# Score masks off TensorE, part of the normalising on GpSimd, and small matmuls between the first transposes, in a kernel of two attention and token-mixing layers

## The chip, the cores and the metric

The kernel runs as one program on one core of a Trainium2 chip. The metric is device time in microseconds, the median of the runs shown. Five engines work side by side: TensorE (PE in the profile, its weight loads apart as PEld), VectorE (DVE), ScalarE (ACT), GpSimd (POOL) and SyncE (SP), which here only issues DMAs. Each takes its own instructions strictly in order, and they wait for one another by semaphores.

## The reference, cut to what matters

```python
def _A_ref(x, wqkv, wo):                      # B=1, S=2048, D=512
    H = 32; Dh = 16; W = 256
    q, k, v = split(x @ wqkv)                 # (B, H, S, Dh) each
    scores = einsum("bhqd,bhkd->bhqk", q, k) * Dh ** -0.5
    mask = (i - j >= 0) & (i - j < W)         # causal, window of 256 keys
    p = softmax(where(mask, scores, -1e9))
    return reshape(einsum("bhqk,bhkd->bhqd", p, v)) @ wo
def _B_ref(x, w1, b1, w2, b2):                # mixes along the 2048 tokens; F = 1792
    u = gelu(einsum("bsd,sf->bdf", layernorm(x), w1) + b1)
    return transpose(einsum("bdf,fs->bds", u, w2) + b2)
for _ in range(2):                            # the same weights both times
    x = x + _A_ref(layernorm(x), A_wqkv, A_wo)
    x = x + _B_ref(layernorm(x), B_w1, B_b1, B_w2, B_b2)
```

Everything arrives as bf16. There are 32 heads of 16 columns, so a score matmul uses few rows of the array.

## The kernel before, in words

The 2048 tokens are 16 tiles of 128 rows that stay in SBUF. For attention, each layer goes through chunks of queries (layer 0: two of 256 queries, then three of 512; layer 1: four of 512), and through four groups of eight heads in each.

**A score group** (`f_sc`, L710) is the unit of the attention stage: some 8 to 24 small matmuls that fill four PSUM banks (two tiles of two banks). ScalarE then takes the exponential in two instructions (L736, "exp"), which write the probabilities to one of seven tiles of `pt`. A layer has 76 score groups, numbered 0 to 75 here, and so 152 exps. Blocks on the edge of the window hold scores that must not count. They are dealt with in one of two ways: GpSimd multiplies the probabilities by 0 or 1 after the exp (`f_mask`, L757), or TensorE adds a large negative bias to the scores before it, by extra matmuls of a selector with a bias table (L721). `BIASED` says which groups take the second way: in layer 0 two of each five groups in chunk 2 and in chunk 3, and eight of the ten groups in chunk 1; in layer 1 none. Then come the products with V ("PV", `f_pv`, L774, one per several score groups and 64 to 96 matmuls each), VectorE's transpose of the result (L794), the reciprocal (L798), a product with it on VectorE or GpSimd (L800), a second transpose (L805), the output projection and the residual (L816).

**Before attention** each pair of tiles is normalised: statistics (`stat` L492, `agg` L494) on VectorE, the power -1/2 on GpSimd (`rstd` L505), and the normalising itself (`normalise`, `xh`, L512) on VectorE. In layer 0 the first four tiles are transposed by TensorE (L570), evicted (`evt`, L577 on VectorE or L579 on ScalarE), and projected to K, Q and V (L534, a line shared by all the plain matmuls). K is spread into a zero-padded layout: from PSUM (`evka`, L602 on ScalarE or L603 on VectorE) in the first chunk, later by way of a staging tile (`evk` L614 or L616, then `kz`: L629 on GpSimd or VectorE, or eight DMAs at L624). The other tiles are transposed by DMA (`tr`, L563).

**The token mixing** is dense: `fu` and `ful` matmuls with w1 (L534 and L895, 128x512), the gelu on ScalarE (L910), `fy` matmuls with w2, and a residual (L936). `u_part` lets a share of the w1 matmuls run while attention goes on, as soon as their tokens have passed attention: they fill TensorE's gaps.

**What sets the order.** The code first makes a list of about 2,400 operations with their dependencies, some with a second or third engine that may take them (`alts`). `ORDER` is a packed list that gives the sequence of all operations and the engine of each; `replay` walks it, hands out buffers in that sequence and fills the engines' queues. So the order within each engine is fixed by `ORDER` alone. PSUM has eight banks in one pool, which score groups, PV sums and all other matmul outputs share.

**The start.** VectorE writes a tile of ones and `f_warm` issues 42 matmuls of 128 columns on it (L395), whose result nobody reads, while the first tokens are loaded.

Of the kernel before, what the change touches and what calls it, by code (L numbers as in the profile page):

```python
# [11 lines left out]
P = 128  # L12
# [15 lines left out]
    'Lc6t+<;M3LzFfBX`U0>1fEJ6AfmuFSET@ZtF)%La7=UrJ2}bqls8$1kBfBekI9yD1IoC9)>}SFOj}XB)>-O&;>=#KQb)_uIFt)O!i_H<nol=i1p%7CTg;_Q0'
    'R<c$%%i19boodag1MYfGvs(2;O5JL;&W8hs*K0x|8jS5K%drEYKECS%lQ^cR_49K_t6C6ZHqrg*G`PGBdIcD(*Ur_|KQ->yg7K=U8pdW5U)WKkYjLcGmTQS3'
    'Y1ok+;?~ubt{M98&jG)^k^R43se(cm4O(9<mkUbgA|q{8`Jnu6P>x0;H*hDO=eW~yOrW#SEK!i<e7-39L=mLw!SPO_I-R2YvUibQ;=EVIdEmO^F&=l_K~|=e'  # L30
    'h6%<7fr!}k_%@Dx&#hkgLCaq{#72&72SH5;RW)l?P1p5=*t%{IP=D)r)Kgs7kY)Ws5RZrsQC(8gFm6Xw9y_)xi(Uu?J2g!)Wzb@A+<>9RDO6~k)l{|sz?*Kj'
    'TQr#f{n{ZIsVtYNyqGT~!Twn~o6g`VoQy@F(QpU`Vdy2jZjx2{{Z<jhu4Q$_TV$gnhwUKsyk@<oyKW^-JvWKH7)Hp}bwg+m)OEpco3_~*L`|+jRfdoPfe^%w'
    'wS{mxxfBm~7Tv5j&AhAteYMi<RVrGaZjHw0<Kb#)>3Ugy^G%)`gP~}g3P_5qAU}XMwBN^;l{gDG-^oeXj^fDr_FLcgEVOZb&oSjc8W2DNA)>SZLZ?PIK;j7l'
    'Qr1ghFHL|@tDV{aAbYckswh+eghG(brY&u}U5oM(!bJiy8YAH(8b#T!*TsLm=vxM8Hd{?SYBZV+N-zYnnYeM1c1$OAfnkV3HUiVqEV+PyF;T;YX%Wj7osI~x'
    'u||Zr!or0s8lTYN8=WwPh{O=l-U(4|ZZH=n<VSd8;UHvwm<T-yhf_9TO!Qbfh@uFtI-M}g$E;H(JPgyc*G(tA-e?rxcGEN|Hk(l1xe3_;j?;7+;sM$1&=!f1'
    '<)9SSGVF%vL%<G9A<eqsIEI0c2*I!o3ur3P02T3LfOata684$+Jlearyrld5>~D|m-*!K&d2&8nPL78p>Evlc@pSJXZ1;co?$^9N*ZmYcsZ`!oo{jH4Pag&='
    'A3tBE@;E8pdV0U)*)gAjl>{r{{(RyG@2?O@$A0jz&(Q{llZ(;Mjy+F~A$ljBoV*C?4JeOMl)xU=hZjl@FRq*(N4$%$a)|R)^al^=kfz72KAObm=Xgc|Ns>N+'
    'VL#(@Qh95pa#E>$5{IS7xSp6LNtMIRBO9e-8t;7`;@?9Gq{r~2iX<JURC=D@r<#yHHChS$s`i^tb9?`jvz2=q9jax|s7I*3c=C9>JS}@8bEo&PL-55Hp9Ao@'
    'bfD5bxCdgtqSS$<(lL^vBq4lMf)nuKcBdR?JN?*~)QMQU7n*xzd8uE*Pd))}7s|6Lsys)ca#U=)%kF!xr=L}h)>Xg(5a}&q+)q5kBos$H?67(Fv}!-Q`;*?i'
    '+YRmp#1DcOT67PCw8u#Vzencu<mBxV1g|EghtpR+0?6y9O64)ehj1$|rMB|AmmHKtdaH`0=jsOzJbAGkNXJ?wN&i#HNv}mvdXQO3l3o&VuO5;FB<WZM_JdD)'  # L40
    '@^Ie6*zxGW@v-~8Ao)*pub+?PztWmVG5>#5{FgB4r{5%j2gDxiS@nEeiho_z{SPfNNM8'
# [52 lines left out]
class Graph:  # L94
# [4 lines left out]
    def __init__(self, nc, es):  # L99
        self.nc = nc  # L100
        self.sem = {e: es.enter_context(nc.semaphore(f"s_{e}")) for e in self.ENGS}
        self.dsem = [es.enter_context(nc.semaphore(f"s_dma{i}")) for i in range(self.NDMA)]
        self.ops = []
        self.last_w = {}
        self.readers = {}

    def op(self, eng, fn, reads=(), writes=(), cost=200.0, prio=None, dma=False, after=(), holds=(), cfg=None, cls=None,
# [20 lines left out]
        for k in writes:  # L128
            w = self.last_w.get(k)
            if w is not None:  # L130
                deps[w.idx] = w
            for rd in self.readers.get(k, ()):
                deps[rd.idx] = rd
        for a in after:
# [170 lines left out]
def bass_interleave_layers__sliding_block__mixer_token_mlp__prompt_kernel(  # L305
# [25 lines left out]
    BIASED = [{1: (0, 1), 2: (2, 4), 3: (2, 4)}, {}]  # L331
# [4 lines left out]
    with es:  # L336
# [679 lines left out]
```

## Time and profile before

| what | us |
|---|---|
| median of 3 runs (444.0 to 444.46) | 444.34 |
| the profiled execution: its time | 445.56 |
| the profiled execution: its span, first to last instruction | 443.6 |
| busy: PE, ACT, DVE, POOL | 418.5, 322.7, 307.4, 201.1 |
| layer 0, attention: from 11 to 159 us, PE busy, ACT busy | 134.93, 143.01 |
| layer 0, token mixing: from 159 to 205 us, PE busy, ACT busy | 45.12, 14.09 |
| layer 1, attention: from 205 to 365 us, PE busy, ACT busy | 155.09, 150.72 |
| layer 1, token mixing: from 365 to 443.6 us, PE busy, ACT busy | 75.24, 11.01 |

Read the table by stage. TensorE is the busiest engine over the whole span, but in layer 0's attention ScalarE is. The mean granted TensorE clock is 0.996 of full speed.

### The profile page before, as it was taken

To read this page: it belongs to the slowest core of one execution; us is meant where nothing else is said; L and a number is where in the kernel's file an instruction comes from. 1 tells how busy PE (TensorE), PEld (TensorE's weight loads), DVE (VectorE), ACT (ScalarE), POOL (GpSimd) and SP (SyncE) were. 2 spreads that over 40 slices of the span, in tenths; PEclk is the share of its full clock that TensorE was granted. 3 is DMA by queue.
4 is the path that set the end of the run, shared out by engine and by line. 5 is a ranking of instruction groups with operands and counts; after the bars stand their busy time and mean duration, and the time that the engine had idled before them with its cause. 6 is when DMAs were issued, how large, how long until landed. Compare 5 with 4: busy or idle time off the path is not lost.

```text
span 443.6 us, 14491 instructions
## 1 busy us (share of the span) xinstructions
PE 418.5 (94%) x6270; PEld 193.5 (44%) x6344; DVE 307.4 (69%) x582; ACT 322.7 (73%) x372; POOL 201.1 (45%) x305
## 2 busy tenths in 40 slices
PE   7888988998999999999999999999999999999997
PEld 5554443443443444444444444444334444444443
DVE  7988879777895678664468789898887457521223
ACT  3999999999999940708989999999999980430000
POOL 3567652464577641001456686677866551000000
PEclk8999999999999999999999999999999999999999
DMA  7575504410133538451434434031211347653533
GB/s 242 153 129 91 101 16 72 77 28 18 36 83 100 122 88 249 125 168 25 99 80 104 111 73 97 17 71 38 56 45 30 105 123 202 189 158 99 167 115 105
DMA packets 94127, 44.47 MB, mean 100 GB/s; under 512 B 24304, under 2 KB 94064, under 8 KB 94064
## 3 DMA queue, kind: packets, MB, share of 16 engines
q1 hardware_dynamic: 94064, 43.55, 39.1%
q8 instruction: 50, 0.82, 0.8%
q14 instruction: 13, 0.11, 0.1%
HBM read 33.56 MB, written 2.10 MB: 80 GB/s over the span
## 4 chain that ended last, share of the span: by engine, by line
PE 79%; ACT 13%; DVE 3%; issue 2%; DMA 1%; SPq 1%; POOL 1%; POOLq 0%
PE PS L534 53%; ACT pt L736 12%; PE PS L710 9%; PE PS L895 8%; PE PS L774 8%; DMA w1b<-in_B_w_dram 1%; DVE rl L794 1%; PE PS L721 1%; DVE stats L492 1%; SPq L830 1%; PE PS L570 0%; DVE vst L649 0%; DVE bb L472 0%; DVE x_sb L816 0%; POOL rstd L505 0%
## 5 line engine op out<-in xcount | busy, mean ns | idle before, releaser
L736 ACT ACTIVATE pt<-PS 128x1024 bf16<-128x1024 f32 (+1 forms) x304 | 281.9, 1034 | 12.0 <-PE PS L710 8.0
L757 POOL TENSOR_TENSOR pt<-pt,ldm 128x256 int32<-128x256 int32 (+2 forms) x226 | 146.9, 675 | 91.7 <-ACT pt L736 91.2
L534 PE MATMUL PS<-xhT,wqkv 128*128 128x512 bf16 (+1 forms) x267 | 65.3, 362 | 4.5 <-issue 1.4
L534 PE MATMUL PS<-xh_sb,w1b 128*128 128x512 bf16 x262 | 66.0, 380 | 2.9 <-issue 1.9
L534 PE MATMUL PS<-uT,w2b 128*128 128x512 bf16 (+1 forms) x285 | 66.7, 370 | 0.8 <-issue 0.5
L710 PE MATMUL PS<-qT,kbd 32*128 32x256 bf16 (+4 forms) x1488 | 60.4, 252 | 5.6 <-ACT pt L736 2.8
L936 DVE SCALAR_TENSOR_TENSOR x_sb<-PS,b2col,x_sb 128x512 bf16<-128x512 f32 x31 | 22.4, 745 | 48.4 <-PE PS L534 48.4
L505 POOL TENSOR_TENSOR rstd<-agg,mhalf 128x2 f32<-128x2 f32 (+1 forms) x33 | 23.5, 713 | 67.8 <-DVE agg L494 67.8
L794 DVE STREAM_TRANSPOSE rl<-PS 128x1024 f32<-128x1024 f32 x32 | 39.9, 1246 | 19.8 <-PE PS L774 19.3
L710 PEld LDWEIGHTS PS<-qT,kbd 32*128 32x128 bf16 x1488 | 22.0, 93 | 63.9 <-ACT pt L736 48.2
L774 PE MATMUL PS<-pt,vb 64*17 64x320 bf16 (+4 forms) x2976 | 43.6, 252 | 1.2 <-DVE vst L649 0.5
L910 ACT ACTIVATE uT<-rl,b1col 128x512 bf16<-128x512 f32 x28 | 18.5, 713 | 36.1 <-DVE rl L906 35.7
L492 DVE BATCH_NORM_STATS2 stats<-x_sb 128x6 f32<-128x512 bf16 x64 | 42.8, 678 | 0.4
L534 PEld LDWEIGHTS PS<-uT,w2b 128*128 128x128 bf16 x294 | 27.1, 98 | 30.9 <-issue 3.7
L534 PE MATMUL PS<-uT,pt 128*128 128x512 bf16 x163 | 39.5, 380 | 0.3
L774 PEld LDWEIGHTS PS<-pt,vb 64*17 64x17 bf16 x2976 | 31.0, 85 | 17.4 <-issue 7.3
L895 PE MATMUL PS<-xh_sb,w1b 128*128 128x512 bf16 x164 | 37.0, 379 | 0.7 <-DMA w1b<-in_B_w_dram 0.6
L534 PEld LDWEIGHTS PS<-xh_sb,w1b 128*128 128x128 bf16 x280 | 23.8, 98 | 31.6 <-issue 7.0
L534 PEld LDWEIGHTS PS<-xhT,wqkv 128*128 128x128 bf16 x288 | 24.5, 99 | 28.8 <-issue 5.6
L534 PE MATMUL PS<-wqkv,xhT 128*128 128x512 bf16 x115 | 32.3, 381 | 3.5 <-issue 1.3
L534 PE MATMUL PS<-wo_sb,oT 128*128 128x512 bf16 x124 | 32.6, 380 | 0.4 <-issue 0.3
L512 DVE TENSOR_SCALAR xh_sb<-x_sb,agg,rstd 128x512 bf16<-128x512 bf16 x64 | 27.2, 445 | 3.2 <-POOL rstd L505 3.1
(64 smaller groups left out, 337.0 us busy)
## 6 DMA issues: line engine op xcount, KB each, us to landing
w1b<-in_B_w_dram SPq DMA_DIRECT2D x112, 128.0 KB, 2.7
w2b<-in_B_w_dram SPq DMA_DIRECT2D x70, 128.0 KB, 2.6
pt<-in_B_w_dram SPq DMA_DIRECT2D x42, 128.0 KB, 3.2
vb<-vst SPq DMA_DIRECT2D x64, 68.0 KB, 2.1
out_dram<-x_sb SPq DMA_DIRECT2D x15, 128.0 KB, 1.8
x_sb<-in_A_x_dram SPq DMA_DIRECT2D x3, 512.0 KB, 7.3
wqkv<-in_A_wqkv_dram SPq DMA_DIRECT2D x4, 256.0 KB, 4.5
wqkv<-in_A_wqkv_dram SPq DMA_DIRECT2D x1, 512.0 KB, 6.6
```

What stands on the lines that cost most here:

```text
L492: op("vector:stat", lambda e: e.bn_stats(st[:, 0:6], x_sb[:, t, :]), reads=[f"x{t}"], writes=[("st", i)], cost=dve_cost(512))
L505: op("gpsimd:rstd", lambda e: e.tensor_tensor(rstd[:, t0:t1, 0], agg[:, t0:t1, 1], mhalf[:, 0:1].to_broadcast([P, t1 - t0]), op=ALU.pow), ...
L512: op("vector:xh", lambda e: e.tensor_scalar(xh_sb[:, t, :], x_sb[:, t, :], agg[:, t, 0:1], rstd[:, t, :], op0=ALU.subtract, op1=ALU.mult), ...
L534: return e.matmul(o, lhsT=w, rhs=x, start=start, stop=stop, skip_group_check=True)
L710: last = e.matmul(bank(tt[r // 2], r % 2)[:, base + c0 * 64:base + (c0 + n) * 64], lhsT=kbd[32 * r:32 * r + 32, tk.slot, o, jj].rearrange( ...
L736: op("scalar:exp", lambda e, ts=ts, tp=tp, i=i, cols=cols: e.activation(probs(tp)[:, i, 0:cols, :], pair(ts)[:, :, 0:cols].rearrange("p r ...
L757: return e.tensor_tensor(v, v, m, op=ALU.mult)
L774: last = e.matmul(bank(t, h)[32 * r:32 * r + 17, i + q0 * 64:i + (q0 + n) * 64], lhsT=vb[64 * h:64 * h + 64, tk.slot, jj, 4 * o + r, :], r ...
L794: op("vector:od", lambda e, t=tod, tr=tr: e.transpose(rl[:, tr.slot:tr.slot + 2].rearrange("p a b -> p (a b)"), pair(t)), reads=[(tod, i) ...
L895: last = e.matmul(bank(tu, tt), lhsT=v()[:, sc - b0, k0 + tt * P:k0 + (tt + 1) * P], rhs=xh_sb[:, sc, :], start=(sc == b0), stop=(sc == NT ...
L910: op("scalar:gelu", lambda e, ft=ft, tt=tt: e.activation(uT[:, ft, :], rl[:, tmps[tt].slot], ACTF.Gelu_apprx_tanh, bias=b1col[:, ft:ft + 1 ...
L936: op("vector:resy", lambda e: e.scalar_tensor_tensor(x_sb[:, t, :], bank(ft), b2col[:, t:t + 1], x_sb[:, t, :], op0=ALU.add, op1=ALU.add), ...
```

## The change

Five edits, all but `ORDER` shown here:

```diff
-    BIASED = [{1: (0, 1), 2: (2, 4), 3: (2, 4)}, {}]
+    BIASED = [{}, {}]
...
         def f_warm(e):
-            for _ in range(42):
+            for _ in range(40):
...
+        def keep_warm(n, after):
+            spare = Tile(banks)
+
+            def f(e):
+                for _ in range(n):
+                    last = e.matmul(PS[:, spare.slot, 0:P], lhsT=uT[:, 0, 0:P], rhs=uT[:, 0, 0:P], start=True, stop=True)
+                return last
+            g.next_pe = [op("tensor:fw", f, reads=["uT0"], writes=[spare], cost=60 * n, cfg="f", cls="f", after=after)]
...
         def normalise(t):
-            op("vector:xh", lambda e: e.tensor_scalar(xh_sb[:, t, :], x_sb[:, t, :], agg[:, t, 0:1], rstd[:, t, :],
-                                                      op0=ALU.subtract, op1=ALU.mult),
-               reads=[f"x{t}", f"ag{t}", f"rs{t}"], writes=[f"xh{t}"], cost=dve_cost(512, 0.25, ptrs=2), lock=True)
+            f_xh = lambda e: e.tensor_scalar(xh_sb[:, t, :], x_sb[:, t, :], agg[:, t, 0:1], rstd[:, t, :],
+                                             op0=ALU.subtract, op1=ALU.mult)
+            op("vector:xh", f_xh, reads=[f"x{t}", f"ag{t}", f"rs{t}"], writes=[f"xh{t}"], cost=dve_cost(512, 0.25, ptrs=2),
+               lock=True, alts=[("gpsimd", f_xh, pool_cost(512, 2))])
...
                    holds=[tx], cfg="f", cls="f")
+                if wide and not layer and m == 0:
+                    keep_warm((2, 8)[i], [g.ops[-1]])
```

`Graph.op` gets `next_pe`, which makes the next TensorE operation follow the small matmuls. With `BIASED` empty, the 352 bias matmuls of L721 go, and the same blocks get 44 more GpSimd masks (L757): 40 of 128x256 and 4 of 128x128.

`ORDER` is new as a whole. It is a compressed list of positions, and unpacked it gives, operation by operation, the sequence and the engine. These are the differences that the prediction speaks of:

| operations | engine before | engine after |
|---|---|---|
| `xh`, 64 in all | 64 VectorE | 29 VectorE, 35 GpSimd (18 of them before the last exp of layer 0) |
| `kz`, 24 | 13 VectorE, 9 GpSimd, 2 SyncE | 13 VectorE, 6 GpSimd, 5 SyncE (layer 0: 4, 7, 1 becomes 8, 1, 3) |
| product with the reciprocal, 32 | 18 VectorE, 14 GpSimd | 16, 16 |
| `evk`, 24 | 23 VectorE, 1 ScalarE | 20, 4 |
| `evka`, 12 | 8 VectorE, 4 ScalarE | 6, 6 |
| `evt`, 8 | 2 VectorE, 6 ScalarE | 3, 5 |
| ScalarE, between the first and the last exp of layer 0, beside the exps | 2 V evictions, 2 Q evictions, 1 `evu` | 2 V evictions, 1 `evka`, 1 `evk`, 1 `evu` |

- TensorE: up to the last score group of layer 0 the same operations in nearly the same places; one `fu` operation (two matmuls of 512 columns) more stands ahead of it, 22 and not 23 behind. In layer 1 operations trade places by one to four groups, and what stands behind its last score group is the same.
- The start: x is loaded tile 0 before tile 1 (before: 1, 0); the load of tiles 2 and 3 moves ahead of the first K weights. GpSimd's memset of the ones in `vst` (L479) moves from between the first two `rstd` to behind the two after them, and a memset of `kbd` (L482) moves ahead of the first `rstd`. The second of the two first evictions `evt` goes to VectorE.
- GpSimd, score groups 5 to 17 of layer 0: before, 13 masks, 3 `rstd`, 3 products, 2 `kz` and a memset of 128x2048; after, 10 of those masks, 8 added ones of 128x256 and 4 of 128x128, 4 `rstd`, 4 `xh`, 2 products and the memset. The last PV of chunk 1 stands behind score group 17, the mask it reads last (of group 15) just ahead of it in the unpacked sequence.
- SyncE in layer 0: `kz` 3 and 7 stand one behind the other, ahead of two w1 loads, the first transpose for the last quarter of the tokens, and the w1 load that the first `fu` reads; `kz` 6 stands behind three more transposes and two V transfers and is read by score group 46.

More of the change, by code (lines that the diff above doesn't have):

```diff
@@ new lines @@
+    'i#;#8j_Yf~1O6@eaJ%%qn~&^U+c2)NUaX8&6ix8rg)^3=>BW)^2Yt9Cpa*(tE-7M`f&P>}w3e&OT$0k%G0n+jZVs)9B}tMp9FIm}XV}LW`x$PgPAl!{&9sr<'
+    '<~NmFIhW&AoRUibrACt8fEy(e>&<$4xs2l)r)#qYh_{WzG_z{u_BPV>5HEyUpcS=oL`404{U^R@n$DL*5(FaEB+CL6OzBsaD>*}Jv)Qc4YUPlnA}tJG^OoNA'
+    'H3dUolF3A<sH$b!?Y6D{R5$D|iTy`GsBJbe)-)Ag8aUW&yq9awEeZl8$5vF1AVulPva0Gruct_|))jbE$b~TGMQMGz;?p#Ra+ap+)pFUqT3#)0Ha9Q%O_Hpp'
+    '{N!pfA!I>*JpIeaomN$KJSvJ|!53sw*rvTu7Yn=B@Atc1Xm_^7-@4=OsIWVoKMe=cIPZ0&!C>V3?FRjxb=sY5JZ`r$BSV5K%W@a#JjO|qWLZ10VOGb@n|xzg'
@@ new lines @@
+    'pH)!<RgJJVt)oy?s}aV?g}$c}C)P+<dB?Jle7U&1^o<!e#ZZUvg`o~qPV2OlJeRq4yUqDcKWJr1IrThW)52*{DI6z7sFBz<C#$aSxrSl9CwKzVb)Is>Sm3h3'
+    '!M6mcsmm!w+-yA7H9SJR*w;GUj%w$5Zrg<Cc~OXCLC`dw*Z8XMZ|Np!a}KWi4eU6sfgyy3t`F&KP1l`V6(oTdMP5V#<ax>^e&aX_t%#~fw{!k2tFW(4N!na%'
+    'Q(l><%49Nus;2TnpGKN($_O;kbh-d(0|EernW&CCohATG-pN~l;{ZtNkW(dzz6BgjFRLW3$I<5U2)PI-jc81c(+FUgsOdBuP(~c(I0TsJmSyR>X_$^dI2D2@'
+    'GUSl@0~NKA(Uojjv`j%TMIB>9nCqe@sqOl3I25uh^L+(M6uKHUjmMQ%rIJ=KuGj0YY}=;W;RShM@1jGFV!{_o9uo8chh#*JbDGT;pdqwYFDZHI5T!2~<tQ4x'
@@ L42 @@
+    'zq7IIY43n#pZ0<G?Qm?sL)^nY&o|4QXL9$BWp|x$^f_k7Fz3F2d5S)JCk6lpe0v=pEciX!kN&6G`#PPg&^M6h*t-s5%iz8`EPVo}COeF>cl}oW<{HdFrSATJ'
+    'cm$p~!Flw7%#%INfFD43WF$Oqt5WHnH@m0OKAqCNs4#n%r<$=;Lc7ryXK@ZRWgqqA^M^9S-qY+Z<5T{}TRP$So_Z%3r~oq09uf$`hdq7F@(z^aEggIYAcT)8'
+    'u+Nw&-R*lXA!piLI+nKd_!xL3M|WCt*gAV)%G09DJ{Flh4(Cs2B)%{Fw;WFg$Foxnoay17atvV3H0kxn-0Nic$vp0*;6Bh%Q%)Lj2zvCnS4D;?pIV$bboH5<'
+    'o~E4~PBOxP|9Eh}$<hC2iu}OgoNsRg)c?&+GJg8G@l>wg5u)$i{tZ@5TA}'
 )
@@ L105, in __init__ @@
         self.readers = {}
+        self.next_pe = []
     def op(self, eng, fn, reads=(), writes=(), cost=200.0, prio=None, dma=False, after=(), holds=(), cfg=None, cls=None,
@@ L133, in op @@
                 deps[rd.idx] = rd
+        if eng == "tensor":
+            after, self.next_pe = list(after) + self.next_pe, []
         for a in after:
```

41 lines of the change are left out of this document (15 added, 26 removed).

## The prediction

> **What bounds the kernel now.** I read the windows by stage first, then the waits of ScalarE in the first stage, the start in the timeline, and last the groups that the change touches. Windows by stage (PE, PEld, DVE, ACT and POOL busy, granted clock, DMA share, GB/s):
>
> ```profile
> 11.00:159.00 148.00, 134.93 (x2921) 64.31 (x2950) 118.09 (x229) 143.01 (x159) 87.54 (x126) 1.00 0.37 77
> 159.00:205.00 46.00, 45.12 (x308) 21.02 (x312) 32.32 (x62) 14.09 (x22) 3.77 (x6) 1.00 0.55 155
> 205.00:365.00 160.00, 155.09 (x2615) 66.57 (x2645) 119.40 (x213) 150.72 (x173) 104.78 (x158) 1.00 0.30 73
> 365.00:443.60 78.60, 75.24 (x358) 35.31 (x362) 29.25 (x50) 11.01 (x16) 1.51 (x2) 1.00 0.52 148
> ```
>
> Layer 0's attention is ScalarE's: 143 of 148 us busy, TensorE 13 us idle. The other three are TensorE's (98%, 97%, 96%). So a matmul that goes from the first stage is worth nothing by itself; it is worth the ScalarE idle time that it causes. ScalarE's waits from 11 to 159 us (us, times, longest) tell how much that is:
>
> ```profile
> ACT pt L736 <- PE PS L721: 2.7, 9, 0.6
> ACT pt L736 <- PE PS L710: 1.7, 4, 1.0
> ```
>
> That is all the idle time ScalarE has there, 4.4 us. Nine exps wait for the bias matmuls, which end a score group. How long those take, in TensorE's timeline (start, length):
>
> ```profile
> 49.95 0.40 PE L710 MATMUL PS<-qT,kbd 32*128 32x64 bf16 x12
> 50.17 0.37 PE L721 MATMUL PS<-bb,sel 32*128 32x96 bf16 x16
> 50.47 1.04 PE L534 MATMUL PS<-xhT,wqkv 128*128 128x512 bf16 x3
> ```
>
> Lengths hold the pipeline's drain; from start to start the 16 take 0.30 us. The start of the kernel, TensorE:
>
> ```profile
> 5.66 0.40 PE L570 MATMUL PS<-ident,xh_sb 128*128 128x128 bf16 x4 [0.60 <-DVE xh_sb L512]
> 6.53 0.40 PE L570 MATMUL PS<-ident,xh_sb 128*128 128x128 bf16 x4 [0.47 <-DVE xh_sb L512]
> 7.60 2.74 PE L534 MATMUL PS<-xhT,wqkv 128*128 128x256 bf16 x12 [0.68 <-ACT xhT L579]
> 10.27 0.62 PE L710 MATMUL PS<-qT,kbd 32*128 32x256 bf16 x12
> ```
>
> and the windows there:
>
> ```profile
> 7.00:7.50 0.50, 0.00 (x0) 0.00 (x0) 0.47 (x3) 0.50 (x1) 0.00 (x0) 1.00 1.05 313
> 7.50:9.00 1.50, 1.40 (x7) 1.03 (x8) 1.24 (x3) 0.37 (x2) 0.00 (x0) 0.53 1.05 337
> 9.00:11.00 2.00, 2.00 (x20) 1.04 (x19) 1.38 (x8) 1.13 (x4) 0.13 (x1) 0.50 1.03 343
> ```
>
> The clock falls to half at 7.5 us and is back at 11. The first 12 projections run at it (2.74/12 = 228 ns; eight of the same form from 10.82 take 1.11 us, 139 ns each), and so does the first score group. The first exp starts at 11.11 us, and from there ScalarE hardly stops until 158.52.
>
> **The change, part by part** (the three windows of the start are on its path, since ScalarE's stage begins there).
>
> *Start, order.* Today a memset (L479, 0.64 us) stands between the two `rstd`; it goes behind them, and the second eviction goes to VectorE (L577 0.40 us for L579 0.58). The memset put ahead (L482, 1.80 us) would fill 2.25 to 4.05 us, when GpSimd waits until 4.31 anyway. That starts the projections some 0.2 to 0.4 us earlier. Against it, eight small matmuls stand behind the second transposes: at the warm-up's 3.96/42 = 94 ns they take 0.75 us, and from some 6.7 us on that is about 7.4, where the evictions end. The two behind the first transposes lie in TensorE's gap of 0.47 us. I take -0.2 us (bounds -0.5 and +0.4).
>
> *Start, clock.* From 4.0 to 7.5 us TensorE is busy 1.86 of 3.5 us, 53%, and then the clock falls. From 17.0 to 20.5 it is busy 2.59 of 3.5, 74%, and it stays. The ten matmuls, less two of warm-up, add 8 x 0.059 = 0.5 us (the end of the warm-up has 17 in its last microsecond) to 8 x 0.094 = 0.75: 67% to 75%. No row lies between, and this is nearer to the row that holds. Held, the 12 projections ahead of the first scores save 12 x 0.089 = 1.07 us, of which 0.75 is on the path (the Q eviction and its semaphore follow the eighth), and the score group 0.62 - 0.40 = 0.2 us (the same form later takes 0.40). I take -0.95 (bounds -0.95 and 0).
>
> Here a page speaks against the edit. The Trainium skill, page "TensorE: Matmul & The Clock Gate", section "HAM oscillation — how this bites in real kernels", says that the clock stays up as long as no idle gap exceeds about 3.4 us. The longest gap in these rows is 0.68 us and the clock fell all the same, so the trace disagrees; by that rule the small matmuls change nothing and the sum would lack the 0.95.
>
> *Bias matmuls.* All 352 go: from start to start 0.30 us for 16, so some 6.5 us of TensorE's 134.9. On the path: nine waits, each shorter by at most the 0.19 (8 matmuls) to 0.30 us that stood ahead: 9 x 0.26 = 2.3. I take -2.3 of the 2.7 (bounds -2.7 and 0). TensorE's other 4 us become idle, for the order moves only one `fu` operation forward; its two matmuls leave the TensorE stage behind, 2 x 0.216 = -0.4 us.
>
> *ScalarE's own work* between first and last exp: before 2.96 us beside the exps (0.60 + 0.47 + 0.64 + 0.62 + 0.63); after 0.60 + 0.84 (`evka`, L602) + 0.60 + 0.59 (L616) + 0.63 = 3.26: +0.3 us.
>
> *Masks on GpSimd.* 40 x 0.752 + 4 x 0.473 = 32 us, 18 `xh` at 0.70 (no such row; nearest L629 on GpSimd, the same shape with one pointer, 700 ns; bounds 0.47, a mask, and 1.06, the product) = 12.6; six `kz` (4.2) and a product (1.06) leave. GpSimd goes from 87.5 to some 127 of 148 us, 86%. No engine but TensorE waits for a mask, at a PV. Today TensorE's weight loads wait 3.1 us for masks, 8 times, over 226 masks; 44 more at that rate: +0.6 us, with the score groups queued behind the PV, and ScalarE behind them (bounds 0 and +5, see the rivals).
>
> *VectorE* loses 18 `xh` at 0.417, an `evk`, an `evka`, gains two Q evictions, four `kz` at 0.441 and a product: about -5 us of 118. It is no bound; nothing on the path is taken from it. The Trainium skill, page "SBUF — State Buffer", section "Who interferes with whom", says that VectorE's `tensor_scalar` in its fast modes and GpSimd lock each other out for a whole instruction. The rows show VectorE as the one that waits: `kz` there takes 253 to 917 ns (median 346), on GpSimd 685 to 782. With GpSimd at 86% for 59%, the 21 `xh` and `kz` left would by that rule lose some 0.27 x 21 x 0.35 = 2 us, less than what left.
>
> *Layer 1.* No mask changes. GpSimd gets 17 `xh`, three products and three `kz` (+17 us on 105 of 160), ScalarE two Q, three K and an `evka` eviction less one `evu` (+2.5 us on 151 of 160). TensorE is the bound and its operations stay. Cost 0 (bounds -2.0, a good third of TensorE's 4.9 us idle, and +2.5, ScalarE's addition in full).
>
> *Sum* against the profiled execution: -0.2 - 0.95 - 2.3 - 0.4 + 0.3 + 0.6 = -2.95. Its 445.56 us (span 443.6 and 1.96 around it) become 442.6; the median of the runs is 1.22 below the profiled one, 444.34, so **441.4 us**.
>
> **The rivals.**
>
> *GpSimd is too full (slower).* In score groups 5 to 17, 13 x 1.94 = 25.2 us (147.4 us of exps over 76 groups), the unpacked order gives GpSimd 10 x 0.665 + 8 x 0.752 + 4 x 0.473 + 4 x 0.72 + 4 x 0.70 + 2 x 1.06 + 1.8 = 24.2 us: 96%. Before, 17.2 by the same rows, and the trace has 17.1 from 21 to 46. At 96% any wait of GpSimd for an exp pushes all masks behind it. The PVs have one to three groups' time of slack; from a lag of about 1.9 us on, each further us stops TensorE at a PV and then ScalarE. If two PVs wait for an `xh`, an `rstd` and a product each (2.5 us), 5 us: 446.4. For it: the 96%. Against: in layer 1 GpSimd carries all masks at 300 to 330 us, 7 to 9 tenths busy, and TensorE waits 2.4 us in the whole stage.
>
> *SyncE holds a transfer back.* A `kz` on SyncE is eight DMAs; six took 5.58 us of its queue, so 7.4 for eight. `kz` 3 and 7 in a row hold it for 15 us from about 55, to 70, and the w1 load of the first `fu` (77.7 us today, 2.7 to land) and `kz` 6 (needed near 98, due near 97) have some 3 us of slack. Late by as much: +3, 444.4.
>
> *The clock still falls.* 53% may not be far below the limit, 74% may be at it. Then +0.95: 442.35.
>
> *Layer 1 gains as well*, 2 us from a freer VectorE: 439.4. For it: TensorE's 4.9 us of idle; against: it waits little for VectorE there.
>
> **How the numbers follow.** Forecast 0.36 (its own range 440.5 to 442.2); clock falls 0.18; layer 1 gains 0.08; SyncE 0.12; GpSimd 0.26 (445.3 to 448). 0.2% is about what a measurement of this kernel can tell from no change: under 443.45 faster, over 445.23 slower. Faster 0.62; the SyncE case 0.12 is the same; slower 0.26. The range runs from 439.0 to 446.8: all but the last of the GpSimd and layer 1 cases.
>
> **What would show it.** Right: a clock of 1.00 throughout 7 to 11 us and a first exp near 10.0; ScalarE idle near 2.7 us up to its last exp, which ends near 156.0; no L721. Wrong: the clock's half windows still there; GpSimd 9 tenths from 21 to 46 us and TensorE waiting for masks by over 2 us; TensorE waiting for w1 near 76 us or score group 46 waiting for a DMA; more than 5 us of TensorE idle in layer 1.

## The result and the profile after

The changed kernel takes 472.62 us (median of 4 runs, 471.0 to 474.44); the kernel before 444.32 us in the same series. The ratio is 1.0639 (95% interval 1.0588 to 1.069): 28.3 us slower, where 441.4 was forecast. The profiled execution took 471.17 us, with a span of 469.4.

First the page of the changed kernel: busy times, the chain that ended last by engine, and two groups (busy us and mean ns of one behind the bar).

```profile
PE 429.2 (91%) x6000; PEld 187.2 (40%) x6000; DVE 301.1 (64%) x539; ACT 325.9 (69%) x378; POOL 300.7 (64%) x380
...
PE 52%; POOL 31%; DVE 7%; ACT 6%; issue 1%; DMA 1%; SPq 1%; DVEq 0%; POOLq 0%
...
L772 POOL TENSOR_TENSOR pt<-pt,ldm 128x256 int32<-128x256 int32 (+2 forms) x270 | 176.2, 682 | 37.0 <-ACT pt L751 36.5
L524 POOL TENSOR_SCALAR xh_sb<-x_sb,agg,rstd 128x512 bf16<-128x512 bf16 x35 | 73.6, 2106 | 1.3
```

GpSimd holds 31% of the chain that ends last, against 1% before. The masks cost what they cost before (682 ns for 675), but one normalisation on GpSimd takes 2.106 us, not the 0.70 that the sum used: 73.6 us in all.

The windows by stage, with the bounds put at this kernel's own first and last exps (columns as in the prediction):

```profile
10.50:171.60 161.10, 140.28 (x2598) 58.23 (x2597) 122.86 (x234) 143.41 (x160) 136.51 (x171) 0.96 0.33 77
171.60:223.70 52.10, 48.35 (x331) 22.09 (x329) 30.62 (x54) 17.10 (x27) 14.86 (x11) 1.00 0.44 125
223.70:385.00 161.30, 153.07 (x2521) 63.18 (x2520) 108.79 (x178) 149.12 (x170) 140.26 (x178) 1.00 0.31 70
385.00:469.40 84.40, 80.05 (x473) 37.21 (x470) 30.83 (x51) 12.89 (x20) 4.06 (x7) 1.00 0.51 144
```

(The last bound is rounded: the last exp ends at 385.28.) By the first and last exps of both, layer 0's attention grew from 147.4 to 161.1 us, the stage behind it from 48.5 to 52.1, layer 1's attention from 154.1 to 161.6, the end from 82.4 to 84.1; the first exp came 0.6 earlier. ScalarE's work in layer 0 is 143.4 us, for 142.4 between the same bounds before; 13 us of new waits stand beside it. The waits of the changed kernel from 10.5 to 171 us, of ScalarE, TensorE and its weight loads:

```profile
ACT pt L751 <- PE PS L725: 16.6, 18, 3.2
...
PE PS L789 <- POOL pt L772: 6.6, 4, 2.5
...
PEld PS L789 <- POOL pt L772: 10.6, 11, 2.8
```

The nine waits for L721 are gone, as forecast. In their place ScalarE waits for scores (L725), which stand in TensorE's queue behind PVs (L789), which wait for masks on GpSimd (L772). One such chain in the timeline of the changed kernel (start, length; GpSimd, TensorE, ScalarE):

```profile
136.33 2.07 POOL L524 TENSOR_SCALAR xh_sb<-x_sb,agg,rstd 128x512 bf16<-128x512 bf16 x1
138.36 2.52 POOL L772 TENSOR_TENSOR pt<-pt,ldm 128x128 int32<-128x128 int32 x4
...
140.94 0.85 PE L789 MATMUL PS<-pt,vb 64*17 64x64 bf16 x40 [2.11 <-POOL pt L772]
141.72 0.61 PE L725 MATMUL PS<-qT,kbd 32*128 32x128 bf16 x12
...
142.38 1.94 ACT L751 ACTIVATE pt<-PS 128x1024 bf16<-128x1024 f32 x2 [2.70 <-PE PS L725]
```

The normalisation holds up four masks for 2.07 us, the PV waits 2.11, and ScalarE 2.70.

Then TensorE's clock falls as well. The granted clock in 40 slices, of the kernel before and of the changed one, and the changed kernel's window from 140 us on:

```profile
PEclk8999999999999999999999999999999999999999
PEclk9989999899997999999999999999999999999999
140.00:150.00 10.00, 6.66 (x83) 2.00 (x84) 3.20 (x6) 3.93 (x5) 9.79 (x9) 0.66 0.00 0
```

By finer windows the changed kernel has 0.50 from 32.0 to 35.4 us, from 90.0 to 93.4 and from 141.2 to 148.0, each time behind a stretch in which TensorE waited; the kernel before stays at 1.00 from 11 us to the end of its attention stages. Half the clock for 13.6 us holds back at most 6.8 us of matmuls. It can be one reason why TensorE is busy 140.3 us in this stage, for 134.3 before, though 352 matmuls are gone. How much of the stage's 13.7 us it makes no run separates.

The start of the changed kernel, VectorE and GpSimd:

```profile
1.89 2.21 DVE L484 TENSOR_SCALAR bb<-tri 32x256 bf16<-32x256 bf16 x1 [0.68 <-POOL tri L456]
...
4.40 0.68 DVE L504 BATCH_NORM_STATS2 stats<-x_sb 128x6 f32<-128x512 bf16 x1
...
2.22 1.81 POOL L494 MEMSET kbd<- 128x2048 f32 x1
```

A VectorE operation of some 0.2 us (0.245 on average in the kernel before) lasts until the memset beside it ends, and the first statistics start at 4.40 (before: 3.24). TensorE's window from 9 to 11 us shows a clock of 1.00 and the first exp comes at 10.50.

### The profile page after: what moved, and what is told of

The parts are those of the page before. It is cut to its first block, busy times and chain, and to the rows that moved or that the text cites. A ratio compares the mean times of both kernels' runs of the same rounds, so it can differ in the third digit from the quotient of the medians.

```text
span 469.4 us, 13943 instructions
## 1 busy us (share of the span) xinstructions
PE 429.2 (91%) x6000; PEld 187.2 (40%) x6000; DVE 301.1 (64%) x539; ACT 325.9 (69%) x378; POOL 300.7 (64%) x380
## 4 chain that ended last, share of the span: by engine, by line
PE 52%; POOL 31%; DVE 7%; ACT 6%; issue 1%; DMA 1%; SPq 1%; DVEq 0%; POOLq 0%
PE PS L547 35%; POOL pt L772 15%; POOL xh_sb L524 12%; PE PS L910 7%; PE PS L725 6%; ACT pt L751 6%; PE PS L789 4%; POOL rstd L517 3%; DVE stats L504 1%; POOL ul L815 1%; DVE bb L484 1%; DMA w2b<-in_B_w_dram 1%; DVE rl L921 1%; ACT uT L925 1%; SPq L857 1%
## 5 line engine op out<-in xcount | busy, mean ns | idle before, releaser
L772 POOL TENSOR_TENSOR pt<-pt,ldm 128x256 int32<-128x256 int32 (+2 forms) x270 | 176.2, 682 | 37.0 <-ACT pt L751 36.5
L524 POOL TENSOR_SCALAR xh_sb<-x_sb,agg,rstd 128x512 bf16<-128x512 bf16 x35 | 73.6, 2106 | 1.3
L547 PE MATMUL PS<-xh_sb,w1b 128*128 128x512 bf16 x280 | 71.6, 391 | 3.0 <-ACT pt L751 1.9
L547 PE MATMUL PS<-xhT,wqkv 128*128 128x512 bf16 (+1 forms) x288 | 68.4, 361 | 3.9 <-DMA xhT<-xh_sb 1.5
L547 PE MATMUL PS<-uT,w2b 128*128 128x512 bf16 (+1 forms) x294 | 68.4, 370 | 0.7 <-DMA w2b<-in_B_w_dram 0.7
L725 PE MATMUL PS<-qT,kbd 32*128 32x256 bf16 (+4 forms) x1488 | 61.3, 255 | 7.5 <-ACT pt L751 3.7
L951 DVE SCALAR_TENSOR_TENSOR x_sb<-PS,b2col,x_sb 128x512 bf16<-128x512 f32 x31 | 22.6, 742 | 54.9 <-PE PS L547 54.7
L789 PE MATMUL PS<-pt,vb 64*17 64x320 bf16 (+4 forms) x2976 | 44.7, 254 | 13.4 <-POOL pt L772 11.8
L725 PEld LDWEIGHTS PS<-qT,kbd 32*128 32x128 bf16 x1488 | 21.8, 93 | 67.7 <-ACT pt L751 44.1
L789 PEld LDWEIGHTS PS<-pt,vb 64*17 64x17 bf16 x2976 | 30.0, 84 | 30.7 <-POOL pt L772 18.1
L910 PE MATMUL PS<-xh_sb,w1b 128*128 128x512 bf16 x168 | 37.4, 379 | 2.5 <-POOL xh_sb L524 2.5
L547 PEld LDWEIGHTS PS<-xh_sb,w1b 128*128 128x128 bf16 x280 | 24.2, 99 | 37.6 <-issue 9.1
L547 PE MATMUL PS<-wqkv,xhT 128*128 128x512 bf16 x128 | 34.6, 381 | 1.0 <-ACT pt L751 0.5
```

The source lines that it names most:

```text
L524: f_xh = lambda e: e.tensor_scalar(xh_sb[:, t, :], x_sb[:, t, :], agg[:, t, 0:1], rstd[:, t, :], op0=ALU.subtract, op1=ALU.mult)
L547: return e.matmul(o, lhsT=w, rhs=x, start=start, stop=stop, skip_group_check=True)
L725: last = e.matmul(bank(tt[r // 2], r % 2)[:, base + c0 * 64:base + (c0 + n) * 64], lhsT=kbd[32 * r:32 * r + 32, tk.slot, o, jj].rearrange( ...
L772: return e.tensor_tensor(v, v, m, op=ALU.mult)
L789: last = e.matmul(bank(t, h)[32 * r:32 * r + 17, i + q0 * 64:i + (q0 + n) * 64], lhsT=vb[64 * h:64 * h + 64, tk.slot, jj, 4 * o + r, :], r ...
L910: last = e.matmul(bank(tu, tt), lhsT=v()[:, sc - b0, k0 + tt * P:k0 + (tt + 1) * P], rhs=xh_sb[:, sc, :], start=(sc == b0), stop=(sc == NT ...
```

## The experiments

Theory A: the price of one normalisation on GpSimd is what costs. Rival B: the masks that TensorE gave up fill GpSimd's queue. Rival C: the new order itself is worse, whatever the operations last.

**E4, the price by itself.** GpSimd alone runs seven forms of the operation, eight each, on 128x512 bf16. It does not compute the reference. E6 adds further forms, and VectorE beside GpSimd; it does not compute the reference either.

```diff
+e.tensor_scalar(y, x, m, r, op0=ALU.subtract, op1=ALU.mult)      # L37
+e.tensor_scalar(y, x, r, m, op0=ALU.mult, op1=ALU.add)           # L39
+e.tensor_scalar(y, x, m, 2.0, op0=ALU.subtract, op1=ALU.mult)    # L41
+e.tensor_scalar(y, x, r, 0.0, op0=ALU.mult, op1=ALU.add)         # L43
+e.tensor_scalar(y, x, 0.25, 2.0, op0=ALU.subtract, op1=ALU.mult) # L45
+e.tensor_scalar(y, x, 2.0, 0.25, op0=ALU.mult, op1=ALU.add)      # L47
+e.tensor_scalar(y, x, r, r, op0=ALU.mult, op1=ALU.mult)          # L49
```

> Not the reference's computation: GpSimd alone runs seven forms of its 128x512 bf16 tensor_scalar, eight of each, with no other engine at work; the output is what the first two forms left. It tells what makes xh three times as long as the K spread (0.70 us). If it is contention with VectorE, subtract with two pointers takes 0.7 to 0.9 us here too. If it is the second pointer, all three two-pointer forms take some 2.1 us. If it is the subtraction, the three forms with it take 2.1 and multiply-add with two pointers 0.7 to 0.8.

The groups of E4 (the last number ahead of the second bar is ns of one):

```profile
L37 POOL TENSOR_SCALAR y<-x,v 128x512 bf16<-128x512 bf16 x8 | 16.5, 2077 | 8.6 <-DMA x<-in_A_x_dram 8.6
L41 POOL TENSOR_SCALAR y<-x,v 128x512 bf16<-128x512 bf16 x8 | 15.8, 2007 | 0.0
L45 POOL TENSOR_SCALAR y<-x 128x512 bf16<-128x512 bf16 x8 | 15.2, 1946 | 0.0
L49 POOL TENSOR_SCALAR y<-x,v 128x512 bf16<-128x512 bf16 x8 | 6.1, 804 | 0.0
L39 POOL TENSOR_SCALAR y<-x,v 128x512 bf16<-128x512 bf16 x8 | 6.0, 780 | 0.0
L43 POOL TENSOR_SCALAR y<-x,v 128x512 bf16<-128x512 bf16 x8 | 5.4, 711 | 0.0
L47 POOL TENSOR_SCALAR y<-x 128x512 bf16<-128x512 bf16 x8 | 4.7, 648 | 0.0
```

The three forms with a subtraction take 1.95 to 2.08 us, the four without 0.65 to 0.80, and pointers matter little. The shape and the number of operands, by which the forecast chose its row, were the wrong key; the arithmetic operation decides.

> Not the reference's computation: VectorE and GpSimd run forms alone and side by side; the output is what two of them left. GpSimd alone: add-multiply with two pointers, multiply-subtract, tensor-tensor subtract (bf16, 128x512), the mask's int32 128x256 multiply. If subtraction in a tensor_scalar is slow as such, multiply-subtract takes some 2 us and add-multiply 0.8; if only subtraction in the first place is, multiply-subtract takes 0.8. Then VectorE's fast 128x512 tensor_scalar alone (0.32 expected), beside masks (0.35 to 0.75, if it waits for whole GpSimd instructions), and beside a 128x2048 memset (the first one up to 1.8 us, if a write locks it out too).

E6, GpSimd: L52 adds and multiplies, L54 multiplies and subtracts, L58 masks alone, L61 masks with VectorE busy. VectorE: L40 alone, L43 beside the masks.

```profile
L61 POOL TENSOR_TENSOR q<-z 128x256 int32<-128x256 int32 x24 | 17.2, 751 | 0.5 <-DVE w L43 0.5
L54 POOL TENSOR_SCALAR y<-x,v 128x512 bf16<-128x512 bf16 x8 | 16.5, 2073 | 0.0
...
L52 POOL TENSOR_SCALAR y<-x,v 128x512 bf16<-128x512 bf16 x8 | 6.0, 767 | 13.9 <-DVE w L40 13.9
L58 POOL TENSOR_TENSOR q<-z 128x256 int32<-128x256 int32 x8 | 5.5, 723 | 0.0
...
L43 DVE TENSOR_SCALAR w<-x,v 128x512 bf16<-128x512 bf16 x16 | 10.9, 758 | 36.9 <-POOL q L58 36.9
...
L40 DVE TENSOR_SCALAR w<-x,v 128x512 bf16<-128x512 bf16 x16 | 5.3, 405 | 3.8 <-DMA x<-in_A_x_dram 3.8
```

x + (-m) costs 767 ns where x - m costs 2077, so the price can be taken away with the work kept. A minus behind the multiplication (L54) is as dear as one ahead of it. And side by side it is VectorE that waits (405 to 758 ns), while GpSimd's masks hardly do (723 to 751).

**E2 and E10: the move alone, in the order before.** E2 puts the same 35 `xh` on GpSimd in the kernel before, and changes nothing else.

```diff
-            op("vector:xh", lambda e: e.tensor_scalar(xh_sb[:, t, :], x_sb[:, t, :], agg[:, t, 0:1], rstd[:, t, :],
+            op(("gpsimd" if n_xh[0] - 1 in ON_POOL else "vector") + ":xh",
+               lambda e: e.tensor_scalar(xh_sb[:, t, :], x_sb[:, t, :], agg[:, t, 0:1], rstd[:, t, :],
```

> The kernel before, with the same 35 normalisings put on GpSimd and nothing else changed (bias matmuls, order and warm-up as before). Theory A: 35 x 2.1 = 73 us more for GpSimd, in an order that never reckoned with it, so 15 us or more slower, 460 to 480 us. Theories B and C: near the 444.3 us of before, at most 450.

481.06 us, ratio 1.0824 (1.0805 to 1.0843): 36.7 us slower, one `xh` at 2100 ns. E10 is E2 with the addition, its mean's sign turned by a small VectorE operation behind each mean:

```diff
+            op("vector:neg", lambda e: e.tensor_scalar(agg[:, t, 0:1], agg[:, t, 0:1], -1.0, 0.0, op0=ALU.mult, op1=ALU.add),
...
-                                                      op0=ALU.subtract, op1=ALU.mult),
+                                          op0=ALU.add, op1=ALU.mult),
```

> The kernel before with the same 35 normalisations on GpSimd as in E2, but as an addition of the turned mean (one small VectorE operation more per block). Theory A (the subtraction's 2.1 us is what costs): most of E2's 36.7 us goes away, 446 to 452. Rival C (an order that was found for other engines costs most, whatever the operation lasts): 455 to 465, with waits for GpSimd's queue as in E3.

453.01, ratio 1.0195 (1.0169 to 1.0221): 28 of the 36.7 us went with the subtraction (one `xh` now 789 ns), a little less than expected.

**E13: the small operation alone.** E10 with all 64 `xh` on VectorE.

```diff
-        ON_POOL = [2, 3, 4, 5, 6, 11, 12, 16, 17, 18, 20, 22, 23, 25, 27, 28, 29, 31, 32, 35, 36, 37, 38, 39, 41, 44, 45, 47, 48, 49, 52, 54, 55, 56, 58]
+        ON_POOL = []
```

> The kernel before with all 64 normalisations left on VectorE, but as an addition of the turned mean, with the small VectorE operation of E10 behind each mean. Nothing runs on another engine. E10, with 35 of them on GpSimd, is 8.6 us above before. If the extra operation (64 of some 0.1 us on a VectorE that is 80% busy) is what costs, 451 to 453; if GpSimd's place in the chain costs, at most 64 x 0.1 = 6.4 us of VectorE's idle time is used up and the time stays at 444.4 to 446.

448.34, ratio 1.0096 (1.0076 to 1.0116): about half of what E10 still lacked (4.15 of 8.6) is that operation. It falls between the two expectations: 64 of 154 ns, each ahead of an `rstd` or an `xh`, are 9.9 us, and some 40% of that comes out at the end. So E5, E8, E9 and E9b below carry a burden that the change does not have.

**E5: the changed kernel with the addition,** else as it is; its edit is that of E10.

> The changed kernel with one thing altered: a small VectorE instruction behind each agg turns the mean's sign (64 more of 128x1), and xh adds it in place of subtracting the mean, on both engines; order and engines as changed. GpSimd alone took 2.08 us for subtract-multiply and 0.78 for multiply-add, so xh on GpSimd should fall to some 0.8 us, what the order reckons with. Theory A (the price of the subtraction is the cause): 440 to 446 us. Theory B (the masks on GpSimd hold up the PVs whatever xh takes, as putting them into the order of before did, 472 us): 455 to 465. If add-multiply is as slow as subtract on GpSimd: 472 or more, and nothing is learnt.

450.45, ratio 1.0134 (1.0116 to 1.0153): 22.2 us of the 28.3 go, with GpSimd's busy time down from 300.7 to 255.9 us. A carries most of it, but the time stays above the 440 to 446 that A gave; the burden of E13 is one part of that.

**E1: the changed kernel with all `xh` back on VectorE,** still subtracting, in the new order.

```diff
+            if o.kind == "xh":
+                alt = 0
```

> The changed kernel with its 35 GpSimd normalisings given back to VectorE, in the same places of the unpacked sequence; all else as changed. Theory A, the price of xh on GpSimd: the changed profile shows 35 of them at 2.106 us (2.062 to 2.224), 73.6 us, where the forecast had 0.70, and GpSimd's queue makes the PVs wait for masks (18.1 + 11.8 us); with them gone the forecast without its +0.6 should come back, 440 to 444 us. Theory B, the 44 added masks fill GpSimd by themselves: 460 us or more. Theory C, the new order and the other moves (K spread on SyncE, evictions) cost as much: 450 to 465 us.

461.95, ratio 1.0406 (1.0353 to 1.0459): only 10.7 us better, and far from the 440 to 444 that A gave. The order was laid out with 29 `xh` on VectorE; with 64 VectorE holds 17% of the chain, and ScalarE waits 22.6 us for scores. That the order does not bear them is a reading, not shown by itself. Going back by engine alone undoes less than half; the expensive operation and the order have to be told apart, as E5 does.

**E3: the masks alone.** The kernel before without the 352 bias matmuls; the 44 masks are put into its order as soon as their exps stand in it.

```diff
-                    on_pe = su[0][0] in biased and len(su) == 1
+                    moved = su[0][0] in biased and len(su) == 1
+                    on_pe = False
...
+            for o in [o for o in left if all(d.idx in seen for d in o.deps)]:
+                order.append((o.idx, 0))
```

> The kernel before, with the 352 bias matmuls left out and the 44 GpSimd masks in their place, each set right behind the second exp of its score group; nothing else changed. Forecast's step: the nine ScalarE waits for L721 go, -2.3 us, and TensorE's waits for masks grow by 0.6: 442 to 443 us. Theory B: the 32 us of masks hold up the PVs, 450 us or more. In between, 444 to 446: the gain and the waits cancel.

472.22, ratio 1.0629 (1.0609 to 1.0649). This looked like B, with GpSimd only 49% busy. The timeline of E3, GpSimd, TensorE and ScalarE, tells what it was:

```profile
30.91 2.10 POOL L758 TENSOR_TENSOR pt<-pt,ldm 128x256 int32<-128x256 int32 x3 [1.27 <-ACT pt L737]
32.96 1.06 POOL L801 TENSOR_TENSOR ul<-rl,rc 128x512 bf16<-128x512 f32 x1
33.95 1.81 POOL L482 MEMSET kbd<- 128x2048 f32 x1
35.72 1.68 POOL L758 TENSOR_TENSOR pt<-pt,ldm 128x256 int32<-128x256 int32 x2
...
37.45 1.26 PE L775 MATMUL PS<-pt,vb 64*17 64x64 bf16 x64 [5.25 <-POOL pt L758]
...
40.14 1.94 ACT L737 ACTIVATE pt<-PS 128x1024 bf16<-128x1024 f32 x2 [5.64 <-PE PS L711]
```

A product and a memset that could have waited stand ahead of two masks that a PV needs; TensorE loses 5.25 us and ScalarE 5.64, and the clock is at half from 37.0 to 43.9 us (0.971 over the whole span). An in-order queue at half load can be late: where a mask stands counts, not how full the engine is.

**E7 and E8: the masks taken out of the changed kernel,** the 352 matmuls back; E7 with the subtraction, E8 with the addition.

```diff
-    BIASED = [{}, {}]
+    BIASED = [{1: (0, 1), 2: (2, 4), 3: (2, 4)}, {}]
```

> The changed kernel with the 352 bias matmuls back and the 44 added masks left out; the new order else, and xh on GpSimd at 2.1 us. The selector's and the bias table's VectorE instructions that the new order has late are drawn ahead of the first score group that needs them. Theory A: the 74 us of xh stay, so still 460 us or more. Theory B: the masks were the cause: 444 to 452.

> Both together: bias matmuls back, and xh by addition. What is left is the new order, the K spread on SyncE, the evictions and the small matmuls. Theories A and B: 441 to 446. Theory C (the order and its transfers cost by themselves): 450 or more.

E7 469.87 (ratio 1.0573, 1.055 to 1.0597), E8 455.1 (1.0238, 1.0203 to 1.0272). With the slow `xh` the masks cost some 2.75 us, just clear of the spread of the two kernels and without the 1.2 us that E7 itself waits for a selector operation that was drawn ahead. With the cheap `xh` they gain 4.65, of which 3.0 is such a wait in E8. With the burden of E13 that wait is why E8 stays above its 441 to 446. E9b has the selector operations in their old places.

**E9 and E9b: the memset, and the mask swap by itself.** E9 is E5 with the memset L494 back behind the first normalisations; E9b is E9 with the bias matmuls back and without the 44 masks.

```diff
+            if g.ops[old[i]] is late_zero:
+                continue
             order.append((old[i], alt))
+            if g.ops[old[i]] is g.last_one:
+                order.append((late_zero.idx, 0))
```

> E5 (new order, xh as an addition) with the memset of kbd on GpSimd moved back behind the first normalisations, where it stood before the change. In E5 and in the changed kernel VectorE's bb operation lasts 2.21 us beside that memset, and the first layer statistics come 1.1 us later than before. Theory A (the memset holds VectorE and its cost passes to the end): 449.7, that is 0.65 to 0.75 below E5 for the same clock at the start; bb near 0.3 us, first statistics near 3.3 us, first exponential 0.65 us earlier than the profile with the same clock. Rival (the transfers of x set the start, the memset costs nothing at the end): 450.45 as E5.

> E9 with the 352 bias matmuls back on TensorE and without the 44 mask multiplications on GpSimd, and with the selector and bias operations where the kernel before had them, so that none of them is waited for as in E8 (3.0 us there). The difference to E9 is the mask swap alone, with a cheap normalisation. The forecast's terms (bias matmuls 2.3 us, masks 0.6) make it 1.7 us slower than E9; E8 against E5 less its one wait makes it 1.6 slower. If GpSimd's masks hold up TensorE even with the cheap normalisation, it is level with E9 or faster.

E9 449.53 (1.0119, 1.0094 to 1.0144), 0.92 below E5, which is within the spread (its four runs go from 448.83 to 451.56, with mean clocks from 1.0 down to 0.992), so the price of the memset is not settled here; `bb` takes 0.47 us in place of 2.21, the statistics start at 2.98 in place of 4.40. E9b 452.72 (1.0186, 1.0168 to 1.0204): with a cheap normalisation the swap gains 3.2 us (2.0 to 3.5 between runs of the same mean clock). B falls: the swap is a loss only behind 2.1 us operations or in a bad place.

**E12 and E14: the start in the kernel before.** E12 adds the warm-up of the change (40 matmuls, then 2 and 8 small ones) and nothing else; E14 adds to it the memset of the ones behind the second `rstd` and the second eviction on VectorE.

```diff
+                if wide and not layer and m == 0:
+                    keep_warm((8, 2)[i], [g.ops[-1]])
```

> The kernel before with nothing but the warm-up of the change: 40 matmuls ahead, and the small matmuls between the first transposes. If they hold the clock (1.00 through 7 to 11 us in the profile, first exponential near 9.9 in place of 11.1), 443.1 to 443.4; if the clock falls or holds from run to run whatever stands there, as E2 and E3 against E5, E7 and E8 have it, 444.0 to 444.6, no difference to before.

> E12 with the start's order of the change and nothing else of it: the memset between the two rstd goes behind them, and the second eviction of the transposes goes to VectorE, ahead of two statistics. By the forecast's step (0.2 us earlier) 443.5; by the first exponential of E9 (9.52 against 9.84) 443.4; if the stage's later waits swallow it, 443.7 as E12.

E12 443.71 over 12 runs, ratio 0.9982 (0.9972 to 0.9993), the one kernel whose interval lies below 1. E14 444.18, ratio 0.9995 (0.9983 to 1.0007): no difference. VectorE has its set-up to do there and copies at 7.47 us, and the first exp comes at 10.19, in E12 at 9.84.

Does the warm-up hold the clock? In the windows from 9 to 11 us:

| start | clock held | clock at about half |
|---|---|---|
| with the small matmuls | the changed kernel, E1, E9, E9b, E12, E14 to E17 | E5, E7, E8 |
| as before | E2, E3, E10, E13 | before |

Each start shows both, though E2 and E3 have the instructions of before up to the first projections, and held starts have their first exp at 9.86 where before has 11.11. The loss costs 1.25 us when it happens. That the small matmuls make it rarer is not shown by 9 of 12 against 4 of 5, but the mean clock that each run lists tells more: 0.996 for the profiled run of before, which lost it at the start and nowhere else in its stages, and 0.999 or 1.0 where the traces show no loss. All 24 runs of E12 and E14 list 0.999 or 1.0, and 26 of the 34 of before beside them, so in the order before the clock held more often with the small matmuls (by chance alone that comes about once in a hundred). For the changed order this does not follow: E16 and E17 (below) list less in 5 of 24 runs, before beside them in 6 of 23. And E12's 0.7 us is not the clock alone: against the runs of before with a full clock (444.27) 0.56 stay, unexplained, and E14 has none of it (444.19 for 444.0).

**E15: the addition without its burden.** E9, with the sign turned by GpSimd itself, right ahead of each of its 35 `xh`, into a buffer of its own; the 29 on VectorE subtract.

```diff
+                op("gpsimd:neg", lambda e: e.tensor_scalar(negm[:, t, :], agg[:, t, 0:1], -1.0, 0.0, op0=ALU.mult, op1=ALU.add),
+                   reads=[f"ag{t}"], writes=[f"ng{t}"], cost=95)
```

> E9 with the mean's sign turned only for the 35 normalisations on GpSimd, by a small GpSimd operation right ahead of each into a buffer of its own; the 29 on VectorE subtract as before, so VectorE has no extra operation and rstd waits for none. If the extra operation costs here what it cost alone (4.15 us in E13), 445.4, and 0.5 to 1 more for 35 small GpSimd operations: 445.4 to 446.4. If GpSimd's place in the chain makes up the rest of E9's distance to before, it stays at 448 to 449.5.

446.66, ratio 1.0065 (1.0041 to 1.0089): 2.3 us above before. The largest ScalarE wait in layer 0 led to this, VectorE and GpSimd of E15:

```profile
11.91 2.11 DVE L485 TENSOR_SCALAR bb<-tri 32x256 bf16<-32x256 bf16 x1
...
11.84 2.11 POOL L495 MEMSET kbd<- 128x2048 f32 x1
```

The memset had only found another victim, once more an operation of the bias table, which nothing reads any more since the bias matmuls are gone. The change left the 12 VectorE operations of the table and its selector standing, and one of them is the operation at the start above.

**E16 and E17: without the dead table.** E16 is E15 without those operations and the small GpSimd memset ahead of them, the large memset back where the change has it; E17 has it as E15 does.

```diff
-            if g.ops[old[i]] is late_zero:
+            if g.ops[old[i]].kind == "sel" or g.ops[old[i]] is first_zero:
                 continue
```

> E15 without the set-up of the bias table and its selector (12 VectorE operations and a GpSimd memset of 128x128), which nothing reads any more once the bias matmuls are gone, and with the memset of kbd back where the change put it, ahead of the first rstd. In E15 one of the table's operations waits beside that memset (2.11 us at 11.91 us in place of some 0.2), a Q eviction stands behind it, TensorE waits 1.47 us and ScalarE 1.29. Theory: that wait goes, 445.4, and the memset ahead now holds nothing, for the statistics read one operand. Rival 1: another operation takes the place of the table's beside the memset, 446.7 as E15. Rival 2: the memset holds the first statistics too, 447.3.

> E16 with the memset of kbd behind the memset of the ones, as in E15. Theory: the next VectorE operation with two operands (the third mask table) waits beside it instead of the bias table's, so that E17 lies between E16 and E15, 445.4 to 446.7. Rival: level with E16, 445.4.

E16 444.35 over 12 runs, ratio 0.9999 (0.9986 to 1.0012): level with before, and 2.3 us below E15, more than expected. E17 445.0 (1.0013, 0.9998 to 1.0028), in between: its trace shows a mask-table operation held for 1.93 us beside the memset. C falls as the main cause: the changed order, with a cheap normalisation and no dead table, is level. It is not free of cost, though. The mask swap is worth 3.2 us by E9b, so a level E16 means that something in the rest of the change takes about as much; what it is was not measured. The waits of ScalarE in E16 from 9 to 157 us, and its end of layer 0 (the table load behind the last exp):

```profile
ACT pt L762 <- PE PS L736: 2.7, 10, 0.5
```

```profile
155.65 1.28 ACT L991 ACT_TABLE_LOAD   x1
```

2.7 us of idle time and a last exp that ends near 156.0 are two of the numbers that the prediction named as its sign of being right; the second comes from a first exp at 9.25, where it had named 10.0.

## Why the prediction was wrong

*The term that failed* is "`xh` at 0.70 (no such row; nearest L629 on GpSimd, the same shape with one pointer, 700 ns; bounds 0.47, a mask, and 1.06, the product)". It measured 2.106, twice its upper bound: 35 of them are 73.6 us of GpSimd, where 0.70 would make 24.5. With 0.70 GpSimd came to 86%, and the waits for masks were taken at the rate of before, 3.1 us and +0.6 (bounds 0 and +5); the weight loads alone now wait 10.6 us for them in layer 0. By the medians the change from the changed kernel to E15, with the addition and the memset moved, takes 25.96 us away, and the one to E16, without the dead table, 2.3 more; nothing of the 28.3 is then left. How the 25.96 divide between subtraction and memset is not measured, for E9's 0.92 lies within the spread. E5's 22.2, with the burden in it, is the least that the subtraction cost.

*The rival "GpSimd is too full"* had the mechanism and not the size. Its account of score groups 5 to 17 with the measured price is 24.2 + 4 x 1.41 = 29.8 us of work in 25.2 us; GpSimd is busy without a break there (10.00 of 10 us from 20 to 30, and again from 30 to 40), and what follows is its chain: mask, PV, score, exp. Its price was 5 us; layer 0 lost 13.7, and the clock that fell three times behind the waits stood in no part of the account. A full queue by itself was no harm: in E16 GpSimd is busy 23.1 of the 26 us from 20 to 46. The rival was set against layer 1, where GpSimd had carried all masks without harm. There it got 17 `xh` as well, and 7.5 us were lost, where "Cost 0" stood.

*Start, order (-0.2):* wrong in sign. The memset would "fill 2.25 to 4.05 us, when GpSimd waits until 4.31 anyway". GpSimd did, but VectorE waited with it: with a held clock the changed kernel's first exp is 0.64 us later (10.50 for 9.86). Without the table it is 0.6 earlier (E16, 9.25), and the statistics beside the memset take their 0.69 us. The Trainium skill, page "SBUF — State Buffer", section "Who interferes with whom", says that VectorE's copies and `tensor_scalar` in two-port modes exclude GpSimd for a whole instruction, and that operations with one input outside them do not; both rows agree. That the other engine blocks in turn does not show in E6, where the masks went from 723 to 751 ns. The prediction cited this rule for the 21 small operations among the masks and overlooked it at the start.

*Start, clock (-0.95):* the price is about right (1.25 us with all that hangs on it), the reason is not. The ten matmuls were to lift the busy share to 67% to 75%. The changed kernel is busy 54% from 4.0 to 7.5 us and held; before had 53% and lost it. The busy share in a window that the reader picks does not decide. The Trainium skill, page "TensorE: Matmul & The Clock Gate", section "What's actually happening", has the clock decided in a free-running window of 3.4 us, whose position against the program varies. The runs agree in that one start gives both outcomes, and in the length: each stretch at half the clock in the traces of before and of the changed kernel lasts 3.4 us or twice that. Where the window stands against the program is not seen in them.

*The step to the median (-1.22)* counts the clock a second time. The profiled 445.56 us belongs to a run that had lost the clock (mean 0.996). In the six series beside the experiments 68 of the 84 runs of before list 0.999 or 1.0, with medians of 444.0 to 444.5, and none of the sixteen with 0.996 is below 444.81. So the 1.22 us that the sum takes off to come down to 444.34 are for the most part the loss that the -0.95 had taken off already; without that term the sum gives 442.35, the figure of its rival "The clock still falls".

*Bias matmuls and masks (-2.3 + 0.6):* right in sign once the queue is free, and too careful: 3.2 us by E9b. In the kernel as changed it was +2.75 (E7).

*VectorE* was "no bound", and is none in the changed kernel, where it holds 7% of the chain. That 5 us of its work leave was worth nothing by itself; E1 suggests that the order counts on it.

*Layer 1 (0):* 154.6 us from first to last exp in E16, for 154.1 before. *SyncE:* no single wait of TensorE's matmuls for a transfer was longer than 1.5 us in the changed kernel; that rival did not happen.

E16 ends level and not at 441.4. By the traces it gains 1.9 us at the start (1.25 of them the clock) and 1.0 in layer 0, and loses 0.5 in layer 1 and 0.9 behind it: 442.1 for 443.6 us of span. The 1.25 are a gain only over that one profiled run of before. Among the runs with a full clock, ten of E16 have a median of 444.26 and 17 of before beside them 444.47: 0.2 us, which is what the other terms leave (0.6 + 1.0 - 0.5 - 0.9).

## What to carry to other kernels

A row prices an operation only on its own engine and with its own arithmetic: where none has it, measure it alone first, or keep the range open above. An engine that work is moved to is a queue in order, so ask what stands ahead of the instruction that others wait for, not how full the engine is. Before a sum goes from a profiled execution to the median, ask what sets the two apart: it may be a term of the sum. And when an edit ends the use of a table, look for what still builds it.

## What the runs showed of the hardware

- A `tensor_scalar` on GpSimd, 128x512 bf16, takes 0.65 to 0.80 us with multiply and add or two multiplies, and 1.95 to 2.08 as soon as it holds a subtraction, in first or second place, by pointer or constant. A `tensor_tensor` subtraction of the same shape took 1.148 us.
- VectorE's `tensor_scalar` of 0.2 to 0.4 us can last until the GpSimd instruction beside it ends: 2.21 us beside a memset of 1.81, 758 ns beside masks of 751. The layer statistics do not (0.69 us beside the memset in E16).
- TensorE's clock after the warm-up holds or falls from one execution to the next with the same instructions: the runs of before list means of 0.996 or of 0.999 and 1.0, 444.81 us and more for the first and medians of 444.0 to 444.5 for the others.
- Where TensorE waits for masks in the attention stage its clock can fall to 0.50, for 3.4 us or twice that: three times in the changed kernel's layer 0, never there in the kernel before.
